# Block attention and feed-forward on one core: x^T of three half-batch pairs by transposing transfers on SyncE's queue in place of TensorE, with a new table of due times

## The chip, the cores and the metric

The kernel runs on one core of one Trainium2 chip. The metric is the device time of one execution in microseconds. Times of single instructions come from one profiled execution.

## The reference

Four batches of eight heads, 768 positions, head size 64, cut into eight blocks of 96. A small 8 x 8 matrix per head is made nearly doubly stochastic by five rounds of exp and row and column sums; it mixes the blocks of k and v. Each block of q then attends to its own mixed block. The output of all heads is x with 3072 rows of 512, and a feed-forward layer follows.

```python
for _ in range(5):
    P = np.exp(P - np.max(P, axis=-1, keepdims=True))
    P = P / (np.sum(P, axis=-1, keepdims=True) + 1e-09)
    P = P / (np.sum(P, axis=-2, keepdims=True) + 1e-09)
k_sorted = np.einsum('bhij,bhjcd->bhicd', P, k_b).reshape(B, H, S, D)
v_sorted = np.einsum('bhij,bhjcd->bhicd', P, v_b).reshape(B, H, S, D)
scores = scale * np.matmul(q_b, k_sb.transpose(0, 1, 2, 4, 3))
attn = softmax(scores)
x = np.matmul(attn, v_sb)            # heads side by side: 3072 x 512
h = np.maximum(x @ w_in, 0.0)        # w_in 512 x 2048
out = h * h @ w_out                  # w_out 2048 x 512, float32 out
```

## The kernel before

**Units.** Attention is done by pairs of heads, four pairs per batch, numbered 0 to 3. The first batch is done in two halves of four blocks each, the others whole. The feed-forward layer is done in eight units of 384 rows, one for each half of a batch: 16 chunks of the up matmul (L993, four matmuls each), a relu on ScalarE (L1001) and a square on VectorE (L1004) per chunk, then three output tiles of four parts each (L1023, four matmuls a part). So a unit has 28 chunks, and unit n starts at chunk 28 n. A unit needs x^T of its half of all four pairs, in the tile xT.

**The stages of a pair.** K and V sort k and v (L622 in the first batch's second half, L586 in the second batch; from the second batch's later pairs on, N and V work on another layout, L757, and Z turns k and q by transposing transfers). S computes the scores and their exp (L665; L655 in the later layout). T turns the sorted v (L721). A multiplies by v (L871) and divides by the row sums on VectorE (L883, L884), into the tile ao, a ring of three. X brings x^T into xT: by four or eight transposes on TensorE (L924) into a PSUM tile xtp and one copy (helper lines 248 on ScalarE and 250 on VectorE), or, from the second batch on for all pairs but one, by one transposing DMA issued on SyncE's (SP's) queue (L906). W and Q prepare the sorting weights and q of the second batch. L prepares a later batch's loads.

**The order.** Nothing is scheduled by the hardware or the tile framework: a planner in the kernel, `Plan`, lists every operation with an engine, a cost in microseconds and what it depends on, and simulates the engines. The instructions of each engine are then issued in the order of the plan. TensorE has two lists, attention and feed-forward, each kept in its own order. The head of the attention list goes first when its due time, counted in feed-forward chunks, has been reached, or when it could start before the next chunk:

```python
if sa is not None and (sf is None or sa < sf - 0.02
                       or (att[0].due <= chunks and sa <= sf + 0.1)):
    pick = (sa, att)
```

The table `DUES` gives the due time of each stage by batch and pair. It also sets the order of the attention list, since the stages are made in the order of their due times; a due time below zero has its effect only through that order. A step that isn't on TensorE takes its place when it is ready. Each change of TensorE's mode (full, by columns, by rows, tiled) is priced at 0.1. A "WAY" is the time from a DMA's issue to its landing, a "DMA" step the time of a load on the transfer engines; neither is an instruction.

**The queues.** POOL issues all loads from HBM, with a cast to bfloat16 (L322): first batch, w_in, then `loads_after`: w_out in four quarters and six halves of the second batch's v, k and q, in the order v, v, k, q, k, q. SP issues the outputs (L972), the way of v through HBM and back (v_way, L781 and L787) and all transposing transfers (L814 and L837 for k and q, L906 for x^T). Before the third and the fourth batch's loads, POOL copies one element of each pair's x^T (held, L1135), which makes the loads wait for the transposes.

Of the kernel before, what the change touches and what calls it, by code (L numbers as in the profile page):

```python
# [18 lines left out]


DUES = {
    (0, "K"): (-130.0, -51.0, -121.0, -51.0),
    (0, "S"): (-63.0, -37.0, -72.5, -31.0),
    (0, "T"): (-110.5, -2.0, -40.5, -38.0),
    (0, "A"): (-47.0, 2.0, -9.5, -15.5),
    (0, "X"): (-8.5, 4.5, 11.0, -2.5),
    (0, "W"): (-102.5,),
    (1, "V"): (4.5, 5.0),
    (1, "Q"): (21.0,),
    (1, "N"): (None, 39.0),  # L30
    (1, "Z"): (None, None, 42.0, 44.5),
    (1, "S"): (26.0, 36.5, 43.0, 47.0),
    (1, "A"): (39.5, 41.0, 44.0, 48.5),
    (1, "X"): (41.0, 41.0, 49.0, 48.5),
    (2, "L"): (49.5,),
    (2, "N"): (57.0, 78.0),
    (2, "V"): (63.5, 89.0),
    (2, "Z"): (68.5, 90.0, 94.0, 91.0),
    (2, "S"): (90.5, 96.5, 99.5, 98.5),
    (2, "A"): (95.5, 96.5, 104.0, 103.5),  # L40
    (2, "X"): (96.5, 99.0, 118.5, 114.5),
    (3, "L"): (124.0,),
    (3, "N"): (138.5, 138.0),
    (3, "V"): (136.0, 143.0),
    (3, "Z"): (144.0, 146.5, 159.5, 156.0),
    (3, "S"): (151.5, 154.0, 160.0, 158.0),
    (3, "A"): (152.0, 156.0, 162.5, 158.0),
    (3, "X"): (162.0, 257.5, 169.0, 366.0),
}


# [133 lines left out]
def kernel(  # L185
# [12 lines left out]
    B, H, S, D = q.shape  # L198
    NB = sort_net.shape[-1]
    BLK = S // NB  # L200
# [3 lines left out]
    HP = H // 2  # L204
# [25 lines left out]
    plan = Plan()  # L230
# [9 lines left out]
    def cost_b(n):  # L240
        return (0.17 + 0.82e-3 * n, 0.15 + 0.53e-3 * n)

    def one_of(eng, cost, fn, deps):
        return plan.add(eng, cost if eng == AD else cost[AD.index(eng)], fn, deps)

    def copy(eng, out, in_):
        if eng == "ACT":
            nc.scalar.copy(out=out, in_=in_)  # L248
        else:
            nc.vector.tensor_copy(out=out, in_=in_)  # L250
# [60 lines left out]
    xT = const.tile([128, KC, n_tok], BF16)  # L311
# [5 lines left out]
    landed = {}  # L317

    def dma(key, mb, dst_src, deps=(), long=True, rate=0.23):
        def issue(e):  # L320
            dst, src = dst_src()
            nc.gpsimd.dma_start(out=dst, in_=src)  # L322
        op = plan.add("POOL", 0.75, issue, deps)
        landed[key] = plan.add("DMA", mb / (0.39 if key[0] == 0 else 0.43 if long else rate), lambda e: None, [op, landed.get("last")])
        landed["last"] = landed[key]
# [3 lines left out]
    def alloc_qkv(b):  # L329
        if b not in qkv:  # L330
            qkv[b] = [ld.tile([128, H, NA * D], BF16, tag=t, name=t) for t in ("qb", "kb", "vb")]

    def in_tiles(b, t, h0):
        return b > 1 and t > 0 or b == 1 and t == 2 or b == 1 and t == 1 and h0 == HP

    def load(b, t, h0, n, p=slice(0, 128), deps=()):
        def dst_src():
            alloc_qkv(b)
            if in_tiles(b, t, h0):
                return (qkv[b][t].rearrange("p (g h) x -> p g (h x)", h=HP)[:, h0 // HP, :],  # L340
                        kv_t[t][b, :, h0 // HP, :])
            return qkv[b][t][p, h0:h0 + n, :], (q_r, k_r, v_r)[t][b, p, h0:h0 + n, :]
        dma((b, t, h0, p.start), 1.57 * n / H * (p.stop - p.start) / 128, dst_src,
            readers[b - 2] + [holds[b]] if b > 1 else list(deps),
            b < 2 and not (b == 1 and t == 0 and h0), 0.25 if b == 1 else 0.37 if t else 0.29)
# [33 lines left out]
    def loads_after(deps):  # L379
        for g in range(4):  # L380
            if g == 1:
                landed["last"] = plan.add("DMA", 0.4, lambda e: None, [landed["last"]])
            t = slice(NT // 4 * g, NT // 4 * (g + 1))
            dma(("w_out", g), 1.05, lambda t=t: (w_out_bf[:, t, :], w_out_r[:, t, :]), deps)
        for t, g in ((2, 0), (2, 1), (1, 0), (0, 0), (1, 1), (0, 1)):
            load(1, t, HP * g, HP, deps=deps)

    rs = const.tile([NH, NB], FP32)
    cs = const.tile([NH, NB], FP32)
# [39 lines left out]
    for it in range(5):  # L429
        step = plan.add("ACT", 0.26, lambda e: nc.scalar.activation(  # L430
            out=p_sb, in_=p_sb, func=AF.Exp), [step])
# [469 lines left out]
        u.nao = nao  # L901

    def s_xt(u, due=0, eng=AD, own=True):
        if u.b > 1 or u.b == 1 and u.hp < HP - 1:
            def turn(e):
                nc.sync.dma_start_transpose(  # L906
                    out=xT[:, u.hp, S * u.b:S * (u.b + 1)].rearrange("p (n q) -> p n q", q=BLK),
                    in_=u.ao.rearrange("p n e d -> p (n e d)"))

            sp = plan.add("SP", 1.4, turn, u.norms)  # L910
            op = plan.add("WAY", 1.3, lambda e: None, [sp])
            rao.use(u.nao, op)
            for hf in u.halves:
                x_done[u.b, u.hp, hf] = op
            return
        st = {}

        ring = r1 if own else rf

        def mm(e):  # L920
            st["p"] = xtp = ((ps1 if own else psf)
                             .tile([128, u.ni, BLK], BF16, tag="p1" if own else "pf", name="xtp"))
            for n in range(u.ni):
                nc.tensor.transpose(  # L924
                    out=xtp[:, n, :],
                    in_=u.ao[:, n, :, :].rearrange("p e d -> p (e d)"),
                    identity=ident[0:96, 0:96])

        def ev(e):
            t0 = S * u.b + BLK * u.i0  # L930
            copy(e, xT[:, u.hp, t0:t0 + BLK * u.ni], st["p"].rearrange("p n q -> p (n q)"))

        s1, old = ring.take()
        pe = plan.add("PE", 0.342 if u.full else 0.17, mm, u.norms + old, due)
        op = one_of(eng, cost_b(BLK * u.ni), ev, [pe])
        ring.use(s1, pe, op)
        rao.use(u.nao, pe)
        for hf in u.halves:
            x_done[u.b, u.hp, hf] = op
# [126 lines left out]
    op = plan.add("DVE", 0.25, p_turn, [step])  # L1066
# [6 lines left out]
    build_w(2, 2, pt, cp, 0, NQ)  # L1073
    builds = [build_w(h0, 4, pt, cp, i0, NQ, "POOL") for h0, i0 in ((4, 0), (0, NQ), (4, NQ))]
    loads_after(builds[-1:])

    us = {}
    for name in FIRST.split():
        stage, n = name[0], int(name[1])
        eng = "ACT" if stage.isupper() else "DVE"  # L1080
        stage = stage.upper()
        if stage == "F":
            f_piece(n)
            continue
        if n not in us:
            us[n] = Unit(0, n, (0,))
            us[n].q_op = qops[n]
        u = us[n]
        own = (name[2:] == "'") ^ (stage in "TX")
        if stage == "K":  # L1090
            u.k_op = s_sort(u, 1, early=True, eng=eng, own=own)
        elif stage == "V":
            u.v_op = s_sort(u, 2, early=True, eng=eng, own=own)
        elif stage == "S":
            s_sc(u)
        elif stage == "T":
            s_vt(u, eng=eng, own=own)
        elif stage == "A":
            s_av(u)
        else:  # L1100
            s_xt(u, eng=eng, own=own)
# [6 lines left out]
              "T": lambda b, hp, due: s_vt(units[b, hp], due),  # L1108
              "A": lambda b, hp, due: s_av(units[b, hp], due),
              "X": lambda b, hp, due: s_xt(units[b, hp], due),  # L1110
              "V": lambda b, g, due: s_nat(b, g, 2, due),
              "N": lambda b, g, due: s_nat(b, g, 1, due)}
# [83 lines left out]
```

The softmax here doesn't subtract the row's maximum and nothing guards it: scores larger than these inputs give would overflow.

## Time and profile before

| What | Value |
|---|---|
| Time, median of 6 runs | 219.64 us (219.45 to 220.06) |
| The profiled execution | 219.97 us |
| Its span in the profile | 218.2 us |
| TensorE busy | 211.4 us, 97% of the span |
| xtp on TensorE (L924) | 40 matmuls of 96 columns, first at 18.6, last at 74.9 us |
| xT<-ao on SP's queue (L906) | 11 transfers, first at 62.9, last at 170.4 us |

The span is the time between the first and the last instruction that the profile shows. PE is TensorE, PEld its weight loads, DVE is VectorE, ACT is ScalarE, POOL is GpSimd, SP is SyncE. A busy TensorE in this profile is one that had a matmul in flight. A slice is one fortieth of the span.

### The profile page before, as it was taken

Reading aid. Unit: us, or ns where it says so; the run is one execution under the profiler, and the core shown is the slowest. Engines: PE = TensorE matmul, PEld = TensorE weight load, DVE = VectorE, ACT = ScalarE, POOL = GpSimd, SP = SyncE. Lnnn points to the kernel's source line nnn. Section 1 sums busy time; section 2 is a strip of 40 time slices with the busy share of each in tenths; the row PEclk is TensorE's granted clock in tenths of the full one; section 3 lists DMA queues with packets and bytes.
Section 4 is the critical chain, followed back from the end, with each engine's and each line's share of the span. In section 5 each row is a group of like instructions: output and inputs, shape, how many; then the busy total and the mean of one; then the engine's idle time right before and its main releaser. Section 6 shows DMA issues by size and latency. Waiting matters only on the chain.

```text
span 218.2 us, 4937 instructions
## 1 busy us (share of the span) xinstructions
PE 211.4 (97%) x1955; PEld 120.5 (55%) x1970; DVE 112.0 (51%) x313; ACT 119.4 (55%) x246; POOL 30.5 (14%) x55
## 2 busy tenths in 40 slices
PE   8989999999999999999999999999999999999994
PEld 3556666446566555445775465435666455456543
DVE  6778667346597437225786045066776155005300
ACT  4656697238943378227874177156865276137421
POOL 7985222200000510000000330000000000000000
PEclk9999999999999999999999999999999999999999
DMA  5999999999953599499771599569994310120012
GB/s 63 195 200 207 206 208 211 204 242 237 197 108 87 95 173 229 72 173 244 203 186 62 123 185 218 117 163 153 246 165 108 98 51 0 48 81 18 0 48 96
DMA packets 46583, 31.21 MB, mean 143 GB/s; under 512 B 26016, under 2 KB 41632, under 8 KB 46560
## 3 DMA queue, kind: packets, MB, share of 16 engines
q0 software_dynamic: 12736, 13.63, 38.4%
q1 hardware_dynamic: 33824, 17.27, 33.6%
q8 instruction: 15, 0.25, 0.4%
q14 instruction: 8, 0.07, 0.1%
HBM read 29.70 MB, written 8.72 MB: 176 GB/s over the span
## 4 chain that ended last, share of the span: by engine, by line
PE 87%; DMA 4%; POOL 3%; DVE 2%; ACT 1%; issue 1%; DVEq 0%; ACTq 0%
PE hp L993 36%; PE op L1023 36%; DMA kb<-in_k_dram 4%; PE p L871 4%; PE p L655 3%; PE p L757 2%; PE op L1051 2%; PE p L665 1%; POOL vb L322 1%; POOL kb L322 1%; PE xtp L924 1%; ACT h L1001 1%; PE p L622 1%; DMA p_sb<-in_sort_net_dram 1%; DVE h L1004 1%
## 5 line engine op out<-in xcount | busy, mean ns | idle before, releaser
L993 PE MATMUL hp<-xT,w_in_bf 128*128 128x384 bf16 x506 | 88.4, 326 | 0.1
L1023 PE MATMUL op<-w_out_bf,h 128*128 128x512 bf16 x353 | 83.7, 379 | 0.9 <-issue 0.2
L1004 DVE TENSOR_TENSOR h<-h 128x384 bf16<-128x384 bf16 x128 | 44.6, 356 | 55.3 <-ACT h L1001 54.4
L1001 ACT ACTIVATE h<-hp 128x384 bf16<-128x384 f32 x128 | 61.8, 495 | 18.3 <-PE hp L993 14.3
L993 PEld LDWEIGHTS <-w_in_bf 128*128 128x128 bf16 x506 | 47.6, 98 | 31.1 <-issue 1.1
L1023 PEld LDWEIGHTS <-h 128*128 128x128 bf16 x368 | 34.3, 98 | 36.9 <-issue 0.9
L248 ACT COPY ob<-op 128x512 f32<-128x512 f32 (+2 forms) x24 | 13.6, 568 | 52.8 <-PE op L1023 50.4
L884 DVE TENSOR_TENSOR ao<-p,rec 96x512 bf16<-96x512 f32 x32 | 22.0, 686 | 1.1
L695 ACT ACTIVATE et<-p 96x384 bf16<-96x384 f32 x40 | 16.8, 488 | 9.2 <-PE p L655 8.9
L871 PEld LDWEIGHTS <-et 96*128 96x128 bf16 x256 | 11.5, 97 | 4.5 <-issue 0.7
L1135 POOL COPY held<-xT 1x3 bf16<-1x3 bf16 (+1 forms) x2 | 0.4, 186 | 78.4 <-DMA xT<-ao 78.4
L883 DVE RECIPROCAL rec<-p 96x8 f32<-96x8 f32 x32 | 6.4, 201 | 8.5 <-PE p L871 8.0
L416 PE MATMUL p<-ones 128*128 128x512 bf16 (+1 forms) x30 | 9.6, 441 | 1.1 <-DVE ones L269 1.1
L250 DVE CAST vn<-p 128x768 bf16<-128x768 f32 x6 | 5.7, 957 | 9.1 <-PE p L757 8.9
L655 PEld LDWEIGHTS <-kx 128*128 128x128 bf16 x80 | 8.5, 144 | 2.4 <-issue 0.4
L871 PE MATMUL p<-vblk,et 96*128 96x65 bf16 x192 | 9.5, 193 | 0.0
L655 PE MATMUL p<-qz,kx 128*128 128x192 bf16 x80 | 9.2, 246 | 0.0
L250 DVE CAST kn<-p 128x768 bf16<-128x768 f32 x5 | 4.8, 958 | 6.4 <-PE p L757 6.4
L322 POOL DMA_DIRECT2D kb<-in_k_dram x10 | 6.4, 637 | 4.4 <-DMA w_in_bf<-in_moe_w_in_dram 2.0
L322 POOL DMA_DIRECT2D qb<-in_q_dram x8 | 6.1, 768 | 4.6 <-DMA w_out_bf<-in_moe_w_out_dram 2.1
L322 POOL DMA_DIRECT2D vb<-in_v_dram x10 | 6.2, 620 | 3.9 <-DMA w_in_bf<-in_moe_w_in_dram 3.9
L685 ACT ACTIVATE et<-p 96x768 bf16<-96x768 f32 x8 | 6.1, 803 | 0.0
(85 smaller groups left out, 126.6 us busy)
## 6 DMA issues: line engine op xcount, KB each, us to landing
out_dram<-ob SPq DMA_DIRECT2D x23, 256.0 KB, 2.1
qb<-in_q_dram POOLq DMA_DIRECT2D x8, 384.0 KB, 11.8
v_way<-vn SPq DMA_DIRECT2D x6, 396.0 KB, 5.3
vblk<-v_way SPq DMA_DIRECT2D x6, 396.0 KB, 4.2
vb<-in_v_dram POOLq DMA_DIRECT2D x6, 384.0 KB, 12.2
kb<-in_k_dram POOLq DMA_DIRECT2D x6, 384.0 KB, 10.9
w_in_bf<-in_moe_w_in_dram POOLq DMA_DIRECT2D x4, 512.0 KB, 12.6
w_out_bf<-in_moe_w_out_dram POOLq DMA_DIRECT2D x4, 512.0 KB, 17.5
```

The lines of the kernel that those rows point to most:

```text
L248: nc.scalar.copy(out=out, in_=in_)
L250: nc.vector.tensor_copy(out=out, in_=in_)
L322: nc.gpsimd.dma_start(out=dst, in_=src)
L416: nc.tensor.matmul(out=p2[slot][:, 0, 0:128 * r].rearrange("p (r x) -> p r x", r=r), lhsT=ones, rhs=ones[:, None, :].to_broadcast([128, r, ...
L655: nc.tensor.matmul(out=scp[:, n // 2, 2 * BLK * (n % 2):2 * BLK * (n % 2 + 1)], lhsT=kx_r[u.kx][:, i::NB], rhs=qz_r[u.qz][:, :, :, C0 * i: ...
L695: nc.scalar.activation(out=et.rearrange("p h x -> p (h x)")[:, HS * h:HS * (h + 1)] .rearrange("p (m c a) -> p m c a", c=C0, a=NA), in_=st ...
L871: nc.tensor.matmul(out=oup[:, h, 66 * n:66 * n + D + 1], lhsT=(et_r[u.et[hf]].rearrange("p h x -> p (h x)") [:, BLK * (2 * n + h):BLK * (2 ...
L884: nc.vector.tensor_tensor(out=u.ao[:, n0:n0 + NQ, :, :].rearrange("p n e d -> p e n d"), in0=ov[:, :, :, 0:D], in1=rec[:, :, :, None].to_b ...
L993: nc.tensor.matmul(out=t["hp", nt][:, 0:HS], lhsT=w_in_bf[:, kc, 128 * nt:128 * (nt + 1)], rhs=xT[:, kc, t0:t0 + HS], start=(kc == 0), sto ...
L1001: nc.scalar.activation(out=t["h1", nt], in_=t["hp", nt][:, 0:HS], func=AF.Relu)
L1004: nc.vector.tensor_tensor(out=t["h2"][:, nt, :], in0=t["h1", nt], in1=t["h1", nt], op=ALU.mult)
L1023: nc.tensor.matmul(out=t["op", mt], lhsT=t["h2"][:, nt, 128 * mt:128 * (mt + 1)], rhs=w_out_bf[:, nt, :], start=(nt == 0), stop=(nt == NT ...
```

## The change

In the first batch's second half, pairs 0, 1 and 2 (not 3) get x^T by a transposing DMA on SP's queue, as most later pairs do already; the slice of xT that is written is now half a batch (96 x 512 elements in). In the plan such a transfer has a way of 6.0 where the later ones have 1.3, and a step of 1.5 is put on the load chain behind the second v half of the second batch; it stands for no instruction. The first half of the first batch, whose order is written out by hand in `FIRST`, is as before. All due times are new.

```diff
--- before.py
+++ after.py
@@ -19,33 +19,33 @@
 
 
 DUES = {
-    (0, "K"): (-130.0, -51.0, -121.0, -51.0),
-    (0, "S"): (-63.0, -37.0, -72.5, -31.0),
-    (0, "T"): (-110.5, -2.0, -40.5, -38.0),
-    (0, "A"): (-47.0, 2.0, -9.5, -15.5),
-    (0, "X"): (-8.5, 4.5, 11.0, -2.5),
-    (0, "W"): (-102.5,),
-    (1, "V"): (4.5, 5.0),
-    (1, "Q"): (21.0,),
-    (1, "N"): (None, 39.0),
-    (1, "Z"): (None, None, 42.0, 44.5),
-    (1, "S"): (26.0, 36.5, 43.0, 47.0),
-    (1, "A"): (39.5, 41.0, 44.0, 48.5),
-    (1, "X"): (41.0, 41.0, 49.0, 48.5),
-    (2, "L"): (49.5,),
-    (2, "N"): (57.0, 78.0),
-    (2, "V"): (63.5, 89.0),
-    (2, "Z"): (68.5, 90.0, 94.0, 91.0),
-    (2, "S"): (90.5, 96.5, 99.5, 98.5),
-    (2, "A"): (95.5, 96.5, 104.0, 103.5),
-    (2, "X"): (96.5, 99.0, 118.5, 114.5),
-    (3, "L"): (124.0,),
-    (3, "N"): (138.5, 138.0),
-    (3, "V"): (136.0, 143.0),
-    (3, "Z"): (144.0, 146.5, 159.5, 156.0),
-    (3, "S"): (151.5, 154.0, 160.0, 158.0),
-    (3, "A"): (152.0, 156.0, 162.5, 158.0),
-    (3, "X"): (162.0, 257.5, 169.0, 366.0),
+    (0, "K"): (-133.5, -48.0, -102.0, -78.0),
+    (0, "S"): (-77.0, -37.5, -97.5, -40.0),
+    (0, "T"): (-99.0, -11.5, -42.0, -63.5),
+    (0, "A"): (-64.0, 16.0, -15.0, -31.5),
+    (0, "X"): (-7.5, 41.5, -9.5, -18.5),
+    (0, "W"): (-100.0,),
+    (1, "V"): (20.5, 30.5),
+    (1, "Q"): (32.0,),
+    (1, "N"): (None, 36.0),
+    (1, "Z"): (None, None, 38.0, 43.5),
+    (1, "S"): (32.5, 40.5, 43.5, 50.0),
+    (1, "A"): (41.0, 41.5, 48.5, 50.0),
+    (1, "X"): (45.0, 41.5, 48.5, 55.0),
+    (2, "L"): (58.0,),
+    (2, "N"): (75.5, 70.5),
+    (2, "V"): (63.0, 88.5),
+    (2, "Z"): (84.0, 84.5, 90.5, 96.0),
+    (2, "S"): (90.0, 96.5, 100.5, 102.0),
+    (2, "A"): (95.0, 98.0, 104.0, 102.5),
+    (2, "X"): (100.0, 101.5, 110.0, 104.0),
+    (3, "L"): (110.5,),
+    (3, "N"): (130.0, 137.5),
+    (3, "V"): (117.0, 140.5),
+    (3, "Z"): (134.5, 143.0, 154.5, 154.0),
+    (3, "S"): (145.0, 150.5, 159.0, 155.0),
+    (3, "A"): (148.0, 153.5, 162.5, 156.5),
+    (3, "X"): (159.0, 248.0, 167.0, 326.0),
 }
 
 
@@ -384,6 +384,8 @@
             dma(("w_out", g), 1.05, lambda t=t: (w_out_bf[:, t, :], w_out_r[:, t, :]), deps)
         for t, g in ((2, 0), (2, 1), (1, 0), (0, 0), (1, 1), (0, 1)):
             load(1, t, HP * g, HP, deps=deps)
+            if t == 2 and g == 1:
+                landed["last"] = plan.add("DMA", 1.5, lambda e: None, [landed["last"]])
 
     rs = const.tile([NH, NB], FP32)
     cs = const.tile([NH, NB], FP32)
@@ -901,14 +903,16 @@
         u.nao = nao
 
     def s_xt(u, due=0, eng=AD, own=True):
-        if u.b > 1 or u.b == 1 and u.hp < HP - 1:
+        early = u.b == 0 and u.halves == (1,) and u.hp < HP - 1
+        if early or u.b > 1 or u.b == 1 and u.hp < HP - 1:
             def turn(e):
+                t0 = S * u.b + BLK * u.i0
                 nc.sync.dma_start_transpose(
-                    out=xT[:, u.hp, S * u.b:S * (u.b + 1)].rearrange("p (n q) -> p n q", q=BLK),
+                    out=xT[:, u.hp, t0:t0 + BLK * u.ni].rearrange("p (n q) -> p n q", q=BLK),
                     in_=u.ao.rearrange("p n e d -> p (n e d)"))
 
             sp = plan.add("SP", 1.4, turn, u.norms)
-            op = plan.add("WAY", 1.3, lambda e: None, [sp])
+            op = plan.add("WAY", 6.0 if early else 1.3, lambda e: None, [sp], tail=5.0 if early else None)
             rao.use(u.nao, op)
             for hf in u.halves:
                 x_done[u.b, u.hp, hf] = op
```

## The prediction, made before the changed kernel was run

> **What bounds the kernel now.** I read the page from its top: busy time, slices, then the chain that ended last.
>
> ```profile
> PE 211.4 (97%) x1955; PEld 120.5 (55%) x1970; DVE 112.0 (51%) x313; ACT 119.4 (55%) x246; POOL 30.5 (14%) x55
> ...
> PE   8989999999999999999999999999999999999994
> ...
> DMA  5999999999953599499771599569994310120012
> ...
> PE 87%; DMA 4%; POOL 3%; DVE 2%; ACT 1%; issue 1%; DVEq 0%; ACTq 0%
> ```
>
> A slice is 5.45 us. DMA is the limit only in the first 20 us or so, where the chain holds its DMA and POOL shares; from 23.3 us, where the feed-forward work begins, TensorE has no empty slice. The transfer engines are nevertheless full from 5 to 60 us: the weights and the second batch come in behind the work. All three removed pieces lie in that time. The view of TensorE's waits after 23 us has one line, 0.2 us long:
>
> ```profile
> PE op L1023 <- issue: 0.2, 1, 0.2
> ```
>
> So what is taken from TensorE's stream there is won, unless something now comes late. The chain between 20 and 80 us (start, length, what) shows the pieces:
>
> ```profile
> 34.63 0.17 PE xtp L924 x4
> 34.80 1.30 PE hp L993 x8
> 36.10 0.17 PE xtp L924 x4
> ...
> 40.86 0.17 PE xtp L924 x4
> ...
> 42.76 0.31 PE p L757 x16
> ...
> 45.22 0.28 PE xtp L924 x4
> ...
> 53.79 0.28 PE p L665 x8
> 54.06 2.71 PE hp L993 x16
> ...
> 56.77 0.28 PE p L665 x8
> ```
>
> By the order of the due times these four xtp are pairs 0, 3, 1 and 2; pair 3 stays. The 0.28 of pair 2 holds about 0.11 for leaving the tiled mode of L757 ahead of it, which its successor will then pay.
>
> **What the Trainium skill says.** "TensorE: Matmul & The Clock Gate", section "Back-to-back issue gap", gives N/2.4 + 2.5 ns for a warm matmul of N columns: 42.5 ns at 96. The trace agrees: 0.17 us for four. "DMA: Bandwidth & Descriptors", section "Issuing engines are not separate DMA queues", says that transfers of SP and of GpSimd run on the same 16 engines and interleave; its section "Queues, rings and completion order", that each engine goes round its queues packet by packet. So a transposing transfer of SP gets in among the loads of POOL at once, but waits for a load's packet at each of its own. The trace agrees for a plain transfer (the v_way write below). Of a transposing one beside loads this trace has no case: the first is issued at 52.50 us, when the last load of the second batch (issued 33.59, 18.3 us to landing) is in.
>
> **The change, part by part.**
>
> 1. Removed: 3 x 4 transposes on TensorE, 3 x 0.17 = 0.51 us, all in its gapless stretch: **-0.51**. Also three copies out of PSUM, 0.36 us on VectorE or 0.48 on ScalarE each. These engines wait for TensorE there, so I count 0 (below 0 by a few tenths if ScalarE, 88% busy from 25 to 35 us, held TensorE's tiles).
>
> 2. Added: three DMA issues on SP and their landing.
>
> ```profile
> v_way<-vn SPq DMA_DIRECT2D x6, 396.0 KB, 5.3
> ...
> xT<-ao SPq DMA_TRANSPOSE x11, 2.8
> ```
> ```profile
> 71.00:72.00 1.00, 1.00 (x12) 0.55 (x11) 0.00 (x0) 1.00 (x3) 0.00 (x0) 1.00 0.43 77
> 72.00:73.20 1.20, 1.20 (x14) 0.72 (x13) 0.92 (x3) 0.46 (x2) 0.00 (x0) 1.00 0.51 100
> ```
> ```profile
> DMA to landing us min/median/max: 8.7/8.7/8.7
> ```
>
> The second fence is the busy time by stretch around one full-size transpose (issued 70.31); the last column but one is the DMA share. The third is the v_way write issued at 44.26 beside the loads. SP has issued nothing between 0.76 and 41.51 us, so 1.2 us of issue for each of three delays nobody; behind them in its queue is the first output at 41.5 us, whose four buffers are free.
>
> Landing: alone a full-size one takes 2.8 us. The v_way write takes 3.4 to 5.3 us without loads and 8.7 with them, an excess of 3.4 to 5.3 for 396 KB; a half-size piece has 98 KB (96 x 512 x 2 bytes) but smaller packets. I take 6 us, between 2.8 and 8.7.
>
> Who waits: the feed-forward unit of the second half (chunk 28) needs all three. Pair 1 is last, its attention output at due 16. Chunk 16 begins at 36.92 now, and stays there within 0.2 (pair 1's L721, 0.22, comes ahead of it, pair 0's transposes go). Then 0.26 for L871, about 1.0 for the norm on VectorE (0.20 + 0.69 and the hand-over): issue at 38.3, landed 44.3 (41.1 to 47.0). Chunk 28 comes after twelve parts of 0.865, the L871 piece and one L757 group (0.31 + 0.16): 36.92 + 10.38 + 0.26 + 0.47 = 48.0. Slack 3.7 us (1.0 to 6.9): **0**. The output tile, in a ring of three, is now held until the landing. Pair 1 takes pair 0's: norm at 30.9, landed 36.9 (33.7 to 39.6), wanted at 37.4. Only at the upper end does VectorE wait, 2.2 us, with no square behind it, for the up half of the unit is done; then pair 1 lands at 49.2, 1.2 late.
>
> 3. What the loads lose. One full-size transpose holds 0.43 x 1.0 + 0.51 x 1.2 = 1.04 us of the sixteen engines, so a half-size one 0.52 and three 1.6. Two are issued before about 38 us. The last quarter of w_out lands at 18.24 + 20.1 = 38.3 and is wanted at 40.0: slack 1.7 against 1.0. The first v half lands at 40.2 and is used at 42.76: 2.5 against at most 1.6. The k and q halves behind (44.0 and 46.8) come up to 1.6 later, but their work moves from 48.95 (chunk 27) to due 32, some 3 us back. **0**, with 0.9 us per piece as the price at which it ends being nothing (1.7/2 at w_out); bounds 0.3 to 1.4 per piece, the latter half of the 2.8 us with the loads wholly blocked.
>
> 4. The filler of 1.5 us behind the second v load exists in the planner alone; it only moves planned work later.
>
> 5. The new due times move nearly everything, so groups of one tile mode are split or joined. From the chain: a score half alone (L665 x8) takes 0.28, plus 0.11 on the matmuls after it; two together 0.45 + 0.11. A split costs 0.22. In the order by due time pair 2's and pair 0's scores part (pair 3's sorting comes between), and so do the sortings of pairs 1 and 3: +0.22 to +0.44, I take **+0.35**. Joined: pair 1's two score halves of the second batch, apart at 53.79 and 56.77 now, come after both p2 slots are free: -0.22; and one N stage of the last batch, in two pieces now (0.59 at 145.68 against 0.31 for one), gets 3 chunks of room on each side: -0.28. Neither is sure; **-0.35** of the 0.50. Further stalls: the chain has some gaps that VectorE's casts cause (around 149 to 153 us, tenths of a us); the order there may mend or make such, 0.3 either way, taken as 0.
>
> 6. Later stages: pair 2's output of the second batch moves from due 44 to 48.5; it ran at about chunk 48 anyway, since its turned k and q come late. Its transposes were issued at 70.31 and landed at 73.1, against the next unit at 76.86; one more chunk (0.87) leaves 2.9. Pair 3's TensorE transposes go one chunk nearer to that unit: one part of 0.865 covers a copy of 0.56 and its hand-over, by about 0.15. The third batch's loads wait for pair 2's landing, so come about 1 us later, and their first use goes from chunk 66 (83.3 us) to dues of 63 to 75: their own lateness sets it. **0**.
>
> **Sum**: -0.51 + 0.35 - 0.35 = -0.51. The profiled execution took 219.97 (span 218.2 and 1.8 around it), 0.33 above the median of 219.64. So it would take 219.46, and the median about 219.1.
>
> **Rivals.**
>
> - *The loads are pushed back* (the slower one). Place: chunk 19, the first to read w_out's last quarter, then the first v half. At 1.4 us a piece, w_out lands at 38.3 + 2.8 = 41.1, 1.1 after 40.0, and all TensorE work stands behind it in order: +1.1 - 0.51 = +0.6, 220.2; at 1.9 a piece +1.6, 221.2. It decides from 0.85 us, and outweighs the saving from 1.1 us. For it: the engines are full (9 in every slice to 60 us), and round-robin turns give a load packet's time to each small packet. Against it: 0.52 us of measured engine time.
> - *x^T comes late.* Chunk 28 waits for pair 1's landing, at the upper end of both landings 1.2 us: 219.64 - 0.51 + 1.2 = 220.3. It needs over 8 us from issue to landing for a quarter of the bytes that took 8.7.
> - *The order eats it.* Splits without the joins: -0.51 + 0.44 = -0.07, 219.6. For it: the new dues of the first batch part these groups on paper already, while each join also needs free tiles and landed data.
> - *More is won than the transposes*: the joins and mended gaps come without the splits: -0.51 - 0.5 - 0.3 = -1.3, 218.3. For it: from 23.29 to the end, 215.22, the feed-forward matmuls need 504 x 0.1625 + 368 x 0.2162 + 3.5 = 165.0 and the attention pieces by their rows about 23.6 (my count), so some 3.3 of the 191.9 us are still small gaps and mode changes.
> - *It doesn't do what it says*: the transposing transfers would be missing from SP's queue before 45 us. The condition names batch 0, second half, pairs 0 to 2, which exist as such units, so I give this nothing.
>
> **How the numbers follow.** 0.2% is 0.44 us, about what a measurement of this kernel can tell from no change. The forecast (218.7 to 219.3) gets 0.43, more won 0.14, the order eats it 0.18, the loads 0.17, late x^T 0.08. Faster by over 0.44: three quarters of the forecast, since it ends 0.1 beyond that limit, and all of "more won", and a little of the order's case, together 0.50. Within: the rest of the forecast and most of the order's case, 0.26. Slower: the two late cases nearly whole and the order's tail, 0.24. Likeliest 219.1; the range 218.4 to 220.6 leaves out the far ends of "more won" and of the loads.
>
> **What would show it.** xtp falls from 40 to 28 matmuls; xT<-ao on SP rises from 11 to 14, the new ones between 30 and 40 us with 5 to 7 us to landing; w_out's last quarter lands by 39.5 and the first v half by 41.8; no wait for a DMA on TensorE or its weight loads at chunk 19 or 28; chunk 28 starts near 48 us. A landing over 8.7 us, or a DMA wait of TensorE over 0.5 us there, makes the forecast wrong; so does an end that moved by more than 0.9 us with nothing late, for then the order, not the transposes, set it.

## The result, and the profile after

| | before | after |
|---|---|---|
| Median of the runs shown | 219.49 us (41 runs) | 218.85 us (20 runs) |
| Profiled execution; its span | 219.97; 218.2 us | 218.68; 216.9 us |

The ratio is 0.9971, with a 95% interval of 0.996 to 0.9982: **0.64 us less** (0.40 to 0.88). The prediction was 219.1 from a median of 219.64, or 0.51 less. Two of the twenty executions after took 224.90 and 226.59 us, where the highest of 41 before was 220.57; the ratio leaves them out, and since no trace of them was kept, their cause is open.

The profiled executions differ by 1.3 us, which must not be taken for the effect. The execution before was 0.48 above its median and began its feed-forward work late: the first sorting of the second half (L624, L622 before) starts at 22.48 us before and 21.95 after, in a stretch where nothing of TensorE's order was changed. The kernel before with the transfers added in its own order (an experiment below) begins it at 22.0, so the late start belongs to that one execution. I therefore compare stretches that begin at that sorting.

The page after: the busy times, the slices, the shares of the chain.

```profile
PE 211.3 (97%) x1942; PEld 120.2 (55%) x1958; DVE 110.0 (51%) x310; ACT 120.7 (56%) x246; POOL 30.4 (14%) x55
...
PE   8999999999999999999999999999999999999994
...
DMA  5999999999983699399992599559997310120012
```

TensorE is as full as before, and its waits after 23 us are now an empty list. What left it is in the view of the tile ao: xtp on TensorE fell from 40 to 28, xT<-ao on SP rose from 11 to 14.

```profile
L928 PE MATMUL xtp<-ident,ao x28: 203/206/217, 18.1 to 74.8; 96*128 96x96 bf16 x28
L910 SPq DMA_TRANSPOSE xT<-ao x14: 1181/1213/1729, 29.4 to 169.3; - x14
...
DMA to landing us min/median/max: 2.8/3.2/8.3
```

The chain between 24 and 50 us shows the work ahead of chunk 28 (start, length, what):

```profile
24.94 0.28 PE p L667 x8
25.22 0.50 PE p L624 x24
...
26.48 0.28 PE p L667 x8
...
28.64 0.50 PE p L624 x24
...
33.53 0.17 PE xtp L928 x4
...
36.78 0.22 PE op L1027
...
43.34 4.48 PE op L1027 x20
47.82 1.30 PE hp L997 x8
```

One xtp is left, pair 3's. The score halves L667 and the sortings L624 stand apart, as the prediction read from the due times. Chunk 28 starts at 47.82 (predicted 48.0), with nothing between it and the matmuls before it.

Cutting both chains at the same feed-forward chunks gives the balance (start in us):

| From / to | before | after | stretch after less before |
|---|---|---|---|
| first sorting of the second half | 22.48 | 21.95 | |
| chunk 16 | 36.92 | 36.78 | +0.39 |
| chunk 56 | 76.86 | 75.89 | -0.83 |
| chunk 112 | 124.95 | 124.09 | +0.11 |
| chunk 168 | 173.66 | 172.53 | -0.27 |
| last output pieces (L1051, L1055 after) | 211.72 | 210.59 | 0.00 |

Chunk 16 starts at the first piece L1023 (L1027 after), the later ones at their first up matmuls. The sum is -0.60 us; the medians differ by 0.64. Of the 1.3 us between the two profiled executions 0.53 are the late start, and 0.16 lie behind the landing of the last output, in the closing semaphore steps.

### The profile page after: what moved, and what is told of

Its sections match the earlier page's. It is cut to its first block, busy times and chain, and to the rows that moved or that the text cites. A ratio compares the mean times of both kernels' runs of the same rounds, so it can differ in the third digit from the quotient of the medians.

```text
span 216.9 us, 4912 instructions
## 1 busy us (share of the span) xinstructions
PE 211.3 (97%) x1942; PEld 120.2 (55%) x1958; DVE 110.0 (51%) x310; ACT 120.7 (56%) x246; POOL 30.4 (14%) x55
## 4 chain that ended last, share of the span: by engine, by line
PE 95%; DVE 2%; ACT 1%; issue 1%; DVEq 0%
PE hp L997 38%; PE op L1027 36%; PE p L418 4%; PE p L873 4%; PE p L657 3%; PE p L759 2%; PE op L1055 2%; PE p L667 1%; PE qtp L538 1%; PE vbp L723 1%; PE p L624 1%; ACT h L1005 1%; PE xtp L928 1%; DVE ao L886 1%; DVE h L1008 1%
## 5 line engine op out<-in xcount | busy, mean ns | idle before, releaser
L1027 PE MATMUL op<-w_out_bf,h 128*128 128x512 bf16 x352 | 83.5, 379 | 0.8
L1008 DVE TENSOR_TENSOR h<-h 128x384 bf16<-128x384 bf16 x128 | 43.9, 356 | 57.8 <-ACT h L1005 57.4
L1027 PEld LDWEIGHTS <-h 128*128 128x128 bf16 x368 | 34.3, 98 | 37.1 <-issue 1.0
L248 ACT COPY ob<-op 128x512 f32<-128x512 f32 (+2 forms) x25 | 14.2, 569 | 51.5 <-PE op L1027 49.1
L418 PE MATMUL p<-ones 128*128 128x512 bf16 (+1 forms) x30 | 10.4, 473 | 1.1 <-DVE ones L269 1.1
## 6 DMA issues: line engine op xcount, KB each, us to landing
qb<-in_q_dram POOLq DMA_DIRECT2D x8, 384.0 KB, 11.5
```

The costliest lines, as they stand in the source:

```text
L418: nc.tensor.matmul(out=p2[slot][:, 0, 0:128 * r].rearrange("p (r x) -> p r x", r=r), lhsT=ones, rhs=ones[:, None, :].to_broadcast([128, r, ...
L1008: nc.vector.tensor_tensor(out=t["h2"][:, nt, :], in0=t["h1", nt], in1=t["h1", nt], op=ALU.mult)
L1027: nc.tensor.matmul(out=t["op", mt], lhsT=t["h2"][:, nt, 128 * mt:128 * (mt + 1)], rhs=w_out_bf[:, nt, :], start=(nt == 0), stop=(nt == NT ...
```

## The experiments

Each kernel is the kernel after with the edit shown, unless it says otherwise; ratios are to the kernel before (the change's own is 0.9971). "First sorting" is the start of the first sorting of the second half (L624 x48; other line numbers in some kernels).

**The due times alone**, with x^T on TensorE in all four pairs.

```diff
-    (0, "X"): (-7.5, 41.5, -9.5, -18.5),
+    (0, "X"): (-7.5, 18.0, -9.5, -18.5),
-        early = u.b == 0 and u.halves == (1,) and u.hp < HP - 1
+        early = False
```

> The new table of due times, but x^T of all four pairs of the first batch's second half on TensorE as before (pair 1's at due 18, behind its attention output). If the twelve transposes themselves make the gain (my theory), this is 0.51 us slower than the changed kernel: about 219.35, ratio to the kernel before 0.999 to 1.000. If the new order makes the gain (rival), it stays near 218.9, ratio 0.997.

Measured: 220.15 us, ratio 1.0023 (1.0009 to 1.0037). TensorE's order is the one after, with three xtp more in its chain:

```profile
36.14 0.17 PE xtp L928 x4
...
36.96 0.17 PE xtp L928 x4
...
39.99 0.17 PE xtp L928 x4
```

From first sorting to chunk 28 it took 26.39 us against 25.87 after: +0.52, three times 0.17, and +0.51 at chunk 56 and chunk 112. So the price of the transposes is **shown**. The whole is slower than the 0.999 to 1.000 expected. In the profiled execution (220.29) the rest of its loss comes from the last batch: the way of v through HBM is read back there in 6.05 us instead of 4.5, and TensorE waits.

```profile
PE p L873 <- DMA vblk<-v_way: 0.8, 1, 0.8
```

Why that read takes longer is open. Its fastest run, 219.23, lies 0.56 above the fastest after (218.67) and level with the fastest before (219.2), as if that wait were missing in it; it has no trace. The order without the transfers wins nothing.

**The transfers alone**, twice. First with the old table, planned anew:

```diff
-    (0, "A"): (-64.0, 16.0, -15.0, -31.5),
+    (0, "A"): (-47.0, 2.0, -9.5, -15.5),
...
```

> The three transposing transfers with the due times of before. My theory: the 0.51 us are won here too, 219.0, ratio 0.9975 to 0.998, unless the q loads, which come about 3 us later beside the transfers, hold up the q and k work of the second batch, which in this table comes early: then up to 219.5. Rival (the order makes the gain): 219.5, ratio 1.000, with nothing late.

Measured: 223.35, ratio 1.0189 (1.0157 to 1.022), above both expectations. The planner turned much of the order about. In the profiled execution, with 225.40 us the longest of six, chunk 28 waited 0.9 us for pair 1, issued at 39.95 with 9.5 us to landing; more waits came in the third batch, around 118 to 121 us.

```profile
PE hp L997 <- DMA xT<-ao: 1.3, 2, 0.9
PE p L873 <- DVE ao L886: 1.2, 2, 0.8
PE op L1027 <- DVE h L1008: 0.9, 1, 0.9
```

Since the plan had moved, this told little about the transfers. So the kernel *before*, its plan and order kept, with the transfers issued behind the norms and the steps of X left without instructions:

```diff
+                if u.b == 0 and u.halves == (1,) and u.hp < 3:
+                    nc.sync.dma_start_transpose(
+                        out=xT[:, u.hp, BLK * NQ:BLK * NB].rearrange("p (n q) -> p n q", q=BLK),
+                        in_=u.ao.rearrange("p n e d -> p (n e d)"))
```

> The kernel before with its own plan and order on every engine, only that pairs 0, 1 and 2 of the first batch's second half get x^T by the transposing transfer, issued behind each norm, in place of their TensorE transposes and copies. If the new due times are only needed to keep pace and net to nothing (my theory: splits +0.34, joins -0.34), this wins the 0.5 us too, 218.95, less a small wait: pair 1 is issued 1.3 us later than in the changed kernel, at 40.2, and lands at 48.4 to 49.5, with chunk 28 at 49.5; q of the second batch lands at 48.8 and is wanted at 48.4. So 218.9 to 219.9. If it stays under 219.0, the new due times bring nothing by themselves; if it is slower than the kernel before, they are what makes the transfers pay.

Measured: 222.50 (median of five; a sixth took 225.35), ratio 1.014 (1.0111 to 1.0169). TensorE's waits in the profiled execution (222.32):

```profile
PE p L871 <- DMA vblk<-v_way: 1.7, 1, 1.7
PE qtp L536 <- DMA qb<-in_q_dram: 1.6, 1, 1.6
```

The first q load of the second batch landed at 49.48, 22.1 us after its issue, and Q stood at its old place ahead of it. My theory that the order isn't needed **fell**: the transfers push the k and q loads back, and the new due of Q (32 in place of 21) is what moves its work behind them. That explains 1.6 us. The other 1.7 are the last read of that way of v, 6.05 us again, and its cause is as open here; how much of it is due to the old order isn't shown.

**What the splits cost.** Two due times moved, which puts pair 0's score half beside pair 2's and pair 1's sorting beside pair 3's:

```diff
-    (0, "K"): (-133.5, -48.0, -102.0, -78.0),
-    (0, "S"): (-77.0, -37.5, -97.5, -40.0),
+    (0, "K"): (-133.5, -77.5, -102.0, -78.0),
+    (0, "S"): (-98.0, -37.5, -97.5, -40.0),
```

> As the changed kernel, with two due times moved: pair 0's scores next to pair 2's (S of pair 0 from -77 to -98) and pair 1's sorting next to pair 3's (K of pair 1 from -48 to -77.5), in the first batch's second half. My theory prices the two splits at 0.34 us by the two chains up to chunk 16: chunk 16 then starts 0.3 to 0.4 us earlier after the first sorting, and the whole takes 218.5 (the planner also reorders some later pieces, 0.2 either way). Rival: the splits cost nothing, since ScalarE's and VectorE's work sets the pace there: chunk 16 unmoved, 218.85.

Measured: 225.32, ratio 1.0271 (1.025 to 1.0291). First sorting to chunk 16 took 14.50 against 14.83: -0.33, as the splits were priced. But the planner, given these, also put the last batch's x^T too late:

```profile
PE hp L997 <- DMA xT<-ao: 3.9, 1, 3.9
```

To part the two, the same moves with the order from chunk 28 on written down from the kernel after:

> The two moves of the run joined again, but with the order of every engine from chunk 28 on written down from the changed kernel, so that the planner reorders nothing there. My theory: the two splits cost 0.34 us, and nothing else changes: 218.5, ratio to the kernel before 0.9955; the start of chunk 28 comes 0.3 us earlier after the first sorting, and all later milestones with it. Rival: what is won up to chunk 16 is lost at chunk 28, since pair 1's x^T sets its start: 218.85.

Measured: 218.62, ratio 0.9958 (0.9945 to 0.9971). Chunk 28 came 25.53 after first sorting against 25.87, and the -0.34 held to chunk 112; at chunk 168 only -0.06 was left, for in the last batch TensorE now waited for ScalarE.

```profile
PE p L958 <- ACT et L782: 0.3, 1, 0.3
```

The split's price stands: 0.34 for two splits. The gain was given back. The same kernel once more, beside the kernel after:

> The run joined_same_rest once more, beside the changed kernel: 0.2 to 0.35 us below it by the theory that the two splits cost 0.34 us and about 0.1 of that is given back in the last batch; at or above it if the first result was the spread of the runs.

> The changed kernel once more, on the same chip as the next one: ratio to the kernel before 0.997, as measured, 0.996 to 0.998.

Measured: 218.67, ratio 0.9961 (0.9947 to 0.9974), and for the kernel after 218.64, ratio 0.9955 (0.9942 to 0.9967). No difference. In the profile of the joined kernel (219.17, the longest of five) w_out's last quarter landed at 39.58 and chunk 19, which reads it, began at 39.62: no slack was left. Of the gain 0.13 was left at chunk 28 and 0.07 at chunk 112, and at chunk 168 it was 0.20 behind. Its first sorting began at 22.2 in both of its profiles, 0.3 later than after; the reason is open.

**How near the edge the landings are.** First pair 3 as well, planned anew:

```diff
-        early = u.b == 0 and u.halves == (1,) and u.hp < HP - 1
+        early = u.b == 0 and u.halves == (1,)
```

> As the changed kernel, with pair 3's x^T by a transposing transfer too. By TensorE's stream alone it wins 0.17 us more: 218.7. By the slack that the changed kernel's profile shows (pair 1's x^T lands at 47.1, chunk 28 starts at 47.8) a fourth transfer in the same queue makes pair 1 land 1.5 to 3 us later, and chunk 28 waits 1 to 2 us: 219.5 to 220.5, with a wait of TensorE for the DMA into xT in its profile.

Measured: 227.25 (median of five), ratio 1.0345 (1.0321 to 1.0368). In the profiled execution, which took 232.77, TensorE waited 6.6 us for x^T, 2.7 of it at chunk 28 and 3.9 in the last batch, where the replanned order is late again. So once more with the order of after kept, pair 3's transfer issued behind its norm and its transposes left away:

> As the changed kernel in every other instruction and its order, but pair 3's x^T too by a transposing transfer (issued behind its norm). TensorE's stream alone: 0.17 us less, 218.7. My theory: the fourth transfer falls between the first and the second in the same queue, so pairs 2 and 1 land 1 to 3 us later; pair 1 landed 0.7 us ahead of chunk 28, which now waits 0.5 to 2.5 us: 219.2 to 221.2, with a wait of TensorE for the DMA into xT.

Measured: 219.50, ratio 0.9999 (0.9984 to 1.0014), which is the whole gain lost. TensorE waited 0.2 us for x^T, under the 0.5 to 2.5 expected; the chain now reaches chunk 28 by the transfer of pair 1:

```profile
37.95 0.70 DVE ao L886
38.64 0.01 issue
38.66 9.20 DMA xT<-ao
47.86 0.04 issue
47.90 1.14 PE hp L1005 x6
```

Chunk 28 came 26.01 after first sorting against 25.87, 0.14 later with 0.17 less work on TensorE, and the 0.14 stayed to the end. The four transfers took 7.5 to 10.1 us each. The 0.14 is less than the 0.65 between the medians. The profiled execution is 0.59 longer than the one after, but its last output landed only 0.12 later, at 216.12; another 0.44 lie behind that landing, in the closing semaphore steps, which took 1.36 us in place of 0.92. Why they did is open, so only 0.14 of the loss is shown to be the fourth transfer.

Then one transfer more, of the same tile into a spare one, ahead of pair 1's:

```diff
+    spare = const.tile([128, NQ, BLK], BF16)
...
+                if early and u.hp in (1,):
+                    nc.sync.dma_start_transpose(out=spare, in_=u.ao.rearrange("p n e d -> p (n e d)"))
```

> As the changed kernel, with one more transposing transfer of the same source into a spare tile issued ahead of pair 1's; it changes no result. If pair 1's landing is within 0.7 us of setting chunk 28's start (my theory), the time grows by what a queued transfer costs less 0.7: landing 1.5 to 4 us later, so 219.7 to 222. If the slack is the 3.7 us of my forecast, nothing changes: 218.85. The k and q loads of the second batch come about 1 us later still; in the profile they are used 2 us after landing now.

Measured: 223.89 (median of five; a sixth, the profiled one, took 226.00), ratio 1.0177 (1.0146 to 1.0207). The chain:

```profile
39.00 0.02 issue
39.01 1.18 SPq L912
40.20 0.04 issue
40.24 11.54 DMA xT<-ao
51.77 0.04 issue
51.82 2.40 PE hp L1000 x7
```

Pair 1 was issued 1.2 us later, behind the added transfer, and took 11.5 us in place of 8.3. Against the kernel after it landed 4.5 us later, counted from first sorting, and chunk 28 came 3.87 later: the difference is, to 0.1 us, the 0.7 of slack that the change has there. And the wait cost more than itself, 5.0 us in the medians and 7.3 between the profiled executions. The busy times by stretch (PE, PEld, DVE, ACT, POOL, granted clock, DMA share, GB/s):

```profile
48.00:51.80 3.80, 0.10 (x1) 0.00 (x0) 0.00 (x0) 0.56 (x1) 0.00 (x0) 0.90 1.20 203
51.80:53.00 1.20, 1.18 (x4) 0.55 (x4) 0.00 (x0) 0.03 (x1) 0.00 (x0) 0.50 1.18 290
...
56.00:57.00 1.00, 1.00 (x5) 0.33 (x3) 0.41 (x2) 0.49 (x1) 0.00 (x0) 0.50 0.33 107
58.00:59.00 1.00, 1.00 (x30) 0.80 (x25) 0.87 (x3) 0.54 (x1) 0.00 (x0) 1.00 1.01 245
```

After 3.72 us of idle TensorE the clock was 0.50 for the next 6.1 us of its work, and seven up matmuls took 2.40 us, 0.34 each against 0.1625. Half of 6.1 is 3 us lost beside the wait (an estimate). The Trainium skill, "TensorE: Matmul & The Clock Gate", section "HAM oscillation — how this bites in real kernels", asks for no idle gaps of TensorE over some 3.4 us. This pause is over that, but here a shorter one is not safe: with four pairs planned anew the 2.69 us before chunk 28 were followed by 2.8 us of work at 0.50, its seven up matmuls again 2.40 us. Two pauses of 1.6 and 1.7 us, in the kernel before with the transfers and its own order, left the clock at 1.00.

**Why a landing takes 8 us.** Theory: the loads. The kernel after with the second batch's six loads held until pair 1's x^T has landed (one run, no interval):

```diff
+                nc.gpsimd.tensor_copy(out=held[0:1, 0:1, 0:1], in_=xT[0:1, 1:2, S - 1:S])
...
+            if early and u.hp == 1:
+                for g in gate:
+                    g.deps.append(op)
```

> As the changed kernel, but the six loads of the second batch are issued only when pair 1's x^T has landed, so that the last transfers have the transfer engines nearly to themselves; the second batch comes late and the time as a whole means nothing. If the loads make the landing long (my theory), pair 1 lands within 2 to 4 us of its issue, where the changed kernel needs 8.2. If it is the half-size form of the transfer or its queue, it stays near 8.

Measured: 234.05 in its one run. The transfers took 7.4 (w_out still coming in), 3.4 and 3.0 us; the last one:

```profile
L916 SPq DMA_TRANSPOSE xT<-ao x1: 1857/1857/1857, 38.9 to 38.9; - x1
...
DMA to landing us min/median/max: 3.0/3.0/3.0
```

The same transfer in the kernel after, issued at the same 38.9 us:

```profile
L910 SPq DMA_TRANSPOSE xT<-ao x1: 1186/1186/1186, 38.9 to 38.9; - x1
...
DMA to landing us min/median/max: 8.3/8.3/8.3
```

So 5.3 of the 8.3 us go when the loads go. Not all of them need be the loads' own: in the kernel after, the second transfer was still on its way (to 43.3) when the third was issued, and here it had landed at 38.6. The first transfer after had no other beside it for 5.8 of its 7.4 us, so some 4.4 us (7.4 less 3.0, an estimate) come from loads alone. Whether any transfer beside loads waits so long, or only the transposing form, is asked by the due times alone plus three plain copies of the same tiles (one run):

```diff
+                if u.b == 0 and u.halves == (1,) and u.hp < 3:
+                    nc.sync.dma_start(out=spares[u.hp == 2], in_=u.ao)
```

> The kernel with the new due times and x^T on TensorE (dues_only), with three plain copies of the same three tiles (96 x 512, 98 KB) into spare tiles issued on SP behind the norms; they change no result. If any transfer of SP beside the loads waits so long, they land after 7 to 8 us like the transposing ones, and the k and q loads come 3 us later (21 us from issue instead of 18). If the many small packets of the transposing form are the cause (my theory: 384 of 256 bytes against 96 of 1 KB), a plain copy lands in 3 to 4.5 us and the loads come at most 1 us later.

```profile
L893 SPq DMA_DIRECT2D spare<-ao x3: 511/512/626, 29.4 to 39.2; - x3
...
DMA to landing us min/median/max: 5.7/6.0/6.0
```

220.25 in its one run. The 6.0 lies between what the two theories gave: beside the same loads the transposing form takes 1.8 to 2.2 us more than the plain one, piece by piece (7.4, 8.1 and 8.3 against 5.7, 6.0 and 6.0). By the packet counts of the pages a transposing transfer is 416 packets, all under 512 bytes, and a plain one 112. That fits the theory of the many small packets, but form and packet count change together here, so which of the two it is stays open. Taking 3.0 for a plain one alone too, which no run shows, the other 3 us would come to any transfer of SP beside these loads.

The loads show the same from their side. Issue to landing of the first k half was 18.2 us with no transfer (due times alone), 19.0 with three plain copies and 21.2 after; of the first q half, in the same order:

```profile
DMA to landing us min/median/max: 17.7/17.7/17.7
DMA to landing us min/median/max: 18.9/18.9/18.9
DMA to landing us min/median/max: 21.1/21.1/21.1
```

## Why the prediction was right

1. **The transposes, -0.51**: right, and shown: 0.51 to 0.52 between the due times alone and the kernel after, at chunks 28, 56 and 112.

2. **The landing, 6 us and 3.7 of slack**: the size failed. Measured 7.4 (pair 0), 8.1 (pair 2) and 8.3 (pair 1), near the upper bound of 8.7 and outside the 5 to 7 that were named as a sign. The prediction took a middle between 2.8 us alone and the 8.7 of a plain write of 396 KB beside loads; the transposing form reaches nearly the same 8.3 with a quarter of the bytes, which the prediction had counted against its rival "x^T comes late". Pair 1 was issued at 38.9 and landed at 47.2, so 0.7 us was left of the 3.7. That the term stayed 0 is luck by this 0.7 us: one more transfer, in the two runs with the order kept, brings the wait about.

3. **The loads, 1.6 us in all**: too small. The first q half took 3.4 us more than with no transfer, 1.1 us a piece against the 0.52 of engine time that the prediction took from the full-size transpose. The critical ones held as predicted: w_out's last quarter landed at 38.2, wanted at 39.63, the first v half at 40.1. The price of 0.9 a piece, from which the step would cost something, lies below these 1.1; w_out lost only 0.8 (issue to landing 20.7 us against 19.9 with the due times alone), probably because little but the first transfer falls ahead of its landing (not shown). The late q half (48.8) was covered, as the prediction put it, by Q's new due: its work starts at 50.84. What that cover is worth shows with the order of before kept: a wait of 1.6 us.

4. **Splits +0.35, joins -0.35**: right in place; the splits right in size, the joins too small at 0.35. To chunk 16 +0.39 was measured; of it 0.34 are splits (pair 1's L723 came ahead, +0.22, and pair 0's xtp went, -0.17), and joining them again gave 0.33 and 0.34. Both joins came: pair 1's two score halves of the second batch now stand as one piece,

```profile
58.70 0.45 PE p L667 x16
```

(-0.22), and the N stage of the last batch that took 0.59 in two pieces is whole (the stretch that holds it -0.27). No run undoes the joins alone, so their price is read from the chains. Not foreseen was one N stage of the third batch that is now in two pieces, and a stretch 0.11 longer:

```profile
90.58 0.53 PE p L759 x16
```

5. **Later stages, 0**: right; TensorE has no wait after 23 us, so nothing there came late, and from chunk 168 on the stretch is the same in both, 38.06 us.

In sum the parts gave -0.60 against -0.51: transposes -0.51, splits +0.34, joins -0.5, the new split +0.11 and rests below 0.1. Of the joins the prediction had taken 0.35 of 0.50; both came whole, and the new split took most of that back, so the near agreement of the sums is in part luck. What the prediction priced only as splits and joins is that the transfers need an order made for them: with the order of before they lose 3.0 us, of which the 1.6 at Q are explained, and the new order alone wins nothing.

## What to carry to other kernels

Moving a small transpose from a full TensorE to the DMA queues wins its TensorE time and no more, and only while the landing has slack at its own, loaded, price: measure that price beside the loads, not alone. Count what the transfers do to the loads as well, and move the loads' first users back by as much. When a due time is changed to measure one thing, keep the order of the rest, or a replanned later stage may hide it.

## What the runs showed of the hardware

- A transposing transfer of 98 KB took 3.0 us from issue to landing with the loads held back and 7.4 to 8.3 beside them; a plain one of the same tile beside them 5.7 to 6.0.
- Three such transfers (416 packets each) delayed the load queue's first q half by 3.4 us, three plain ones (112 packets each) by 1.2.
- A 3.72 us pause of TensorE was followed by 6.1 us of work at half clock, one of 2.69 us by 2.8; pauses of 1.6 and 1.7 us by none.
